# One fused attention and feed-forward kernel on one core: whole result tiles in one transfer, reciprocals on VectorE, one QK tile in batch 0, and another searched order

## The chip, the cores and the metric

The kernel runs on one core of one Trainium2 chip. The time is the device time of one execution in microseconds (us). The core's engines are named as in the profile: PE is TensorE (PEld its weight loads), DVE is VectorE, ACT is ScalarE, POOL is GpSimd, and SP is SyncE, which computes nothing here and issues transfers.

## What is computed

Attention with mixing over the heads ahead of the softmax and behind it, and then a feed-forward layer with a squared ReLU:

```python
scores = scale * np.matmul(q, k.transpose(0, 1, 3, 2))     # 8 batches, 12 heads, 448 x 448, d = 64
scores = np.einsum('bhij,hg->bgij', scores, w_pre)         # 12 x 12
attn = softmax(scores)                                     # max, exp, sum, divide
attn = np.einsum('bhij,hg->bgij', attn, w_post)
attn_out = np.matmul(attn, v)
x = attn_out.transpose(0, 2, 1, 3).reshape(B * S, H * D)   # 3584 x 768
h = np.maximum(x @ w_in, 0.0)                              # 768 x 2048
out = (h * h) @ w_out                                      # 2048 x 768
```

## The kernel before, in words

All matmuls are bf16 and accumulate in eight PSUM banks, the one tile `ps`. A batch passes through these stages, each a chain of PE work and of evictions that ACT or DVE makes:

- **T** (line 833 in batch 0, 837 after it): q and k are transposed on PE and evicted into `qkt`.
- **QK** (975 and 985): 128 query rows of all twelve heads at a time are multiplied with the keys and evicted into `stage`, twelve evictions of 128x448 to a tile. SP then regroups `stage` into `dring` by transfers (`emit_rel`, line 1030): one slot of `dring` is a chunk of ten query rows with its 12 heads, 120 partitions. A batch has 45 chunks, handled in 23 pairs.
- In batch 0 the first `ND = 30` chunks go another way (`emit_spr`, line 916): q is spread out with zeros (`qz`, which lies in `h2t`), and PE makes the chunk directly, with eight matmuls on 32 columns each and one eviction into `dring`. The rest of batch 0's rows are `NQ0 = 2` QK tiles (`QT0`), of 70 and 78 rows, each computed as 128 rows.
- **pre** (1054, 1061, 1069): the pair is mixed with `w_pre`. ACT takes `exp` from PSUM (line 1094) into `pring` and leaves the row sums. A reciprocal of the row sums follows (`t_rec`, 1117 on POOL, where it is a power of -1 with the constant tile `minus1`; 1119 on DVE in the first five pairs), and POOL folds it into the weights of the second mixing (`t_fold`, 1127, `wk2s`).
- **post** (1159): the pair is mixed with `wk2s`; two evictions go into `a2t`.
- **AV** (1216, 1237): times v, evicted into `xt`.
- **F1** (1288, 1296): times `w_in`, then ReLU from PSUM into `h1t` (1333 on ACT, 1334 on DVE), squared by DVE into `h2t` (1343).
- **F2** (1427, 1435, and 1375 for the last two tiles): 128 rows times `w_out`, two evictions into `osb`, and the tile leaves for `out`. The two halves of a tile are 64 positions each, so SP issues one transfer to a half (`fn_od`, line 1473); the last two tiles leave by quarters (1398), some of them issued by ACT.

Every stage but the first may run while others wait: attention of one batch is mixed with F1 and F2 of the batch before. What comes when on PE is a string, `ORDER`. Each character takes the next unit of one stream (0 to 9: T, QK, pre, post, AV, the direct chunks, two streams of F1, two of F2), and characters from a letter on also choose a form. A unit of F1 or F2 can be done with halves of the rows of the array (64x128, two at a time), with the whole array (128x128, half as many matmuls), or with quarters (64x64, twice as many); QK and pre have two forms. `_Plan.run` replays that string against a cost model when the program is built. In it DVE, ACT and POOL take whatever is ready first, evictions go to ACT or DVE by which is free, each PE unit gets the PSUM banks that come free first, a change of form costs `MODE_SWITCH`, and blocks of `BLOCK = 256` PE instructions have to be fetched (`FETCH`). What comes out is a fixed order of instructions on each engine, with semaphore waits; the engines run it in that order. So the constants of the model move instructions, and they cost no time themselves.

At the end the kernel looks whether all row sums were in range (lines 1540 to 1560): three DVE operations, a transfer of 128 numbers (`goods`), a last DVE operation (`flag`). Every engine reads `flag` behind its last task and branches: a second program with a safe softmax follows if the flag is 0 (`emit_engine`).

Of the kernel before, what the change touches and what calls it, by code (L numbers as in the profile page):

```python
# [7 lines left out]
ALU = mybir.AluOpType  # L8
# [14 lines left out]
FETCH = (2700.0, 2300.0, 1500.0)  # L23
# [3 lines left out]
DMA_END = {"move": 1450.0, "load": 1300.0}  # L27
# [3 lines left out]
    "0000511100551155555555555555555c2155555035bcb02515525353c2c5155c1531333355c2555c355332c0"  # L31
    "240443c4b200gh1111h62b3g33hqc31cgc3h2b3hgh3bbbch3633r3gb42444223g1h72qgqb2733g1r12q713h3"
    "6b2673722392003t122j33t2b282bi338333s04202444bb002gqbb28311i313s111s322gh2227hqh3613q1hr"
    "3363q2422444br2br631q1731h613q32h0220gh22qg373r3c38212i3s333814144420022ghh20028118111i1"
    "33s339b22j31t22193229119313t3319242444312q2bq227373163c3631731h2020q1g2br2h236333q20b0r2"
    "r20038318311i33184bb42244229c19311t133t118222833i313s242444232q2b623713733631g12r2br2006"
    "33q33rb17q200262r217293c3t331t2200jc181118133s311842244422391319313t13392422444222838333"
    "i311i31qb2b62qb2622h73733373q1b6rb00h2q0202q22h700239331911j11193182238318331s2424442228"
    "1s311i333814244413bq22g2rb2r23631q32r2br23633g31r002h2633q733r024044412tb2j0209bb2t23811"
    "381138333s11t22jb2922t23831s33i1318b4244422bq2bqb27337631q33731r2q21q2r22h1633673373bs22"  # L40
    "842i2i244422383833s333s22qr6r22293933t33tq4q444hghh6gq7g6hrghisrggh7hg7giqishhjjijtsttsj"
    "j"
# [330 lines left out]
def bass_talking_heads_attention__then__ffn_squared_relu_kernel(  # L373
# [18 lines left out]
    ND = 30  # L392
    NE = 6
    NQ0 = 2
# [21 lines left out]
    with ExitStack() as es:  # L416
# [34 lines left out]
        minus1 = sb("minus1", [128, 2, 1], DT.float32)  # L451
# [41 lines left out]
        def program(guard):  # L493
# [40 lines left out]
            def fn_init(eng, en):  # L534
# [8 lines left out]
                eng.memset(minus1[:, :, :], -1.0)  # L543
# [479 lines left out]
            def emit_rel(b, c, n, r0, d0, nv):  # L1023
# [4 lines left out]
                def fn(eng, en):  # L1028
# [5 lines left out]
                             {SP: (1000.0, 0.0)}, g * 1.0, sem, 16,  # L1034
# [51 lines left out]
            def after_pre(g, t_pre, gr, x):  # L1086
# [28 lines left out]
                def fn_rec(eng, en):  # L1115
                    if en == POOL:
                        return eng.tensor_tensor(rinv[:, p0:p0 + n, :], rowsum[:, g0:g0 + n, :],  # L1117
                                                 minus1[:, 0:n, :], ALU.pow)
                    return eng.reciprocal(rinv[:, p0:p0 + n, :], rowsum[:, g0:g0 + n, :])
# [286 lines left out]
            def emit_F2(b, tile, s, s_F):  # L1406
# [61 lines left out]

                o_free[s] = []
                for x, (p0, n_p, row, step) in enumerate(pieces):  # L1470
                    def fn_od(eng, en, p0=p0, n_p=n_p, row=row, step=step):
                        dst = bass.AP(out.tensor, row * F, [[step * F, n_p], [1, F]])
                        eng.dma_start(dst, osb[p0:p0 + n_p, s, :]).then_inc(sem_out[s].handle, 16)

                    o_free[s].append(plan.add("odma%d_%d_%d" % (b, tile, x), SP, fn_od, evs,
                                              {SP: (720.0, 0.0)}, b * 1000.0 + 710, sem_out[s], 16,
                                              dma=("move", 50.0 + 12.0 * n_p, 200.0)))
# [58 lines left out]
            if not guard:  # L1536
# [26 lines left out]
                t_flag = add("flag", DVE, fn_flag, [t_turn], {DVE: (200.0, 300.0)}, 1e8)  # L1563

# [59 lines left out]
        def emit_engine(eng_name, eng):  # L1624
            tasks = fast[eng_name]
            k = len(tasks)
            while k and tasks[k - 1].name == "final":
                k -= 1
# [3 lines left out]
            with eng.If(fine == 0):  # L1632
                emit_tasks(eng_name, eng, tasks[k:], fast_waits)
# [3 lines left out]
            if k < len(tasks):  # L1637
# [51 lines left out]
```

## Time and profile before

| | us |
|---|---|
| median of 3 runs | 534.45 |
| lowest and highest | 530.79, 538.87 |
| the profiled execution | 531.75 |
| its span, first to last instruction | 530.1 |
| granted PE clock | 0.996 |

| engine | busy us | share of the span |
|---|---|---|
| PE | 504.9 | 95% |
| ACT | 429.9 | 81% |
| DVE | 387.7 | 73% |
| POOL | 292.6 | 55% |

How to read it: the span is 1.65 us shorter than the execution's own time. A busy PE is not a PE at its peak, since the matmuls overlap and their ends are modelled: what a unit really takes is read from the start of one group of matmuls to the start of the next. Idle time "before" a group is what the profile shows as free behind the modelled end of the group ahead of it, so a stall is some tenths of a us longer from start to start than the idle time that is printed. "issue" is time in which an engine waited for nothing that the profile shows.

### The profile page before, as it was taken

The page shows a single profiled execution, that of the slowest core. Times are in us where ns is not written, and L with a number is a line of the kernel's source. Part 1 is how long each engine was busy: PE and PEld are TensorE (multiplying, and loading weights), DVE is VectorE, ACT ScalarE, POOL GpSimd, SP SyncE. Part 2 cuts the span into 40 slices and gives each one's busy share as a digit, 9 for nine tenths or more (in the row PEclk, how much of TensorE's full clock was granted, in tenths as well). Part 3 has the DMA queues.
Part 4 walks back from the last instruction along what each step waited for, and adds up shares of the span by engine and source line. Part 5 has one row for each costly group of instructions (what it writes and reads, how often), then busy time and mean ns, then how long its engine had stood idle before and what let it go on. Part 6 is the DMA issues. An engine that isn't in the chain of part 4 may idle for free.

```text
span 530.1 us, 24988 instructions
## 1 busy us (share of the span) xinstructions
PE 504.9 (95%) x10519; PEld 329.4 (62%) x10519; DVE 387.7 (73%) x816; ACT 429.9 (81%) x1223; POOL 292.6 (55%) x524
## 2 busy tenths in 40 slices
PE   8999999999999999999899989999999999999994
PEld 4446776668765655666566655566666665678862
DVE  7898987889886699867787667776888668555400
ACT  5999989889978798888798878978978878977420
POOL 9847788527944597258752576416964445442000
PEclk9999999999999999999999999999999999999998
DMA  9999999646965799458954699536992567531022
GB/s 165 197 201 172 181 192 183 140 96 138 180 147 117 158 167 185 101 113 155 176 115 96 126 196 151 119 64 146 181 176 55 124 139 145 113 93 35 1 57 70
DMA packets 81811, 71.10 MB, mean 134 GB/s; under 512 B 13610, under 2 KB 78234, under 8 KB 81690
## 3 DMA queue, kind: packets, MB, share of 16 engines
q1 hardware_dynamic: 48138, 46.62, 36.1%
q0 software_dynamic: 33392, 22.59, 31.3%
q8 instruction: 86, 1.41, 1.1%
q14 instruction: 35, 0.29, 0.2%
q10 hardware_dynamic: 160, 0.20, 0.1%
HBM read 45.63 MB, written 11.01 MB: 107 GB/s over the span
## 4 chain that ended last, share of the span: by engine, by line
PE 72%; ACT 15%; POOL 7%; DVE 2%; issue 2%; DMA 1%; ACTq 0%; POOLq 0%
PE ps L1435 23%; PE ps L1296 13%; PE ps L1288 7%; PE ps L1159 7%; ACT pring L1094 6%; PE ps L1069 5%; PE ps L1237 5%; PE ps L985 4%; ACT stage L524 4%; POOL rinv L1117 3%; PE ps L1375 2%; PE ps L1427 2%; ACT dring L524 1%; POOL wk2s L1127 1%; PE ps L975 1%
## 5 line engine op out<-in xcount | busy, mean ns | idle before, releaser
L1117 POOL TENSOR_TENSOR rinv<-rowsum,minus 128x2 f32<-128x2 f32 (+1 forms) x179 | 126.1, 706 | 174.7 <-ACT pring L1094 173.9
L1094 ACT ACTIVATE pring<-ps 128x448 bf16<-128x448 f32 x360 | 192.3, 562 | 12.0 <-PE ps L1069 9.4
L525 DVE CAST a2t<-ps 128x480 bf16<-128x480 f32 (+1 forms) x205 | 124.8, 641 | 31.6 <-PE ps L1159 30.6
L1435 PE MATMUL ps<-w_out_sb,h2t 64*128 64x384 bf16 (+1 forms) x1728 | 141.4, 323 | 0.5 <-issue 0.4
L525 DVE CAST stage<-ps 128x448 bf16<-128x448 f32 (+1 forms) x193 | 115.0, 617 | 25.8 <-PE ps L985 15.1
L1296 PE MATMUL ps<-xt,w_in_sb 64*64 64x448 bf16 (+4 forms) x1872 | 121.0, 327 | 1.8 <-issue 1.2
L524 ACT ACTIVATE a2t<-ps 128x480 bf16<-128x480 f32 (+1 forms) x163 | 87.6, 581 | 22.5 <-PE ps L1159 21.7
L1435 PEld LDWEIGHTS ps<-w_out_sb,h2t 64*128 64x128 bf16 (+1 forms) x1728 | 74.6, 97 | 45.1 <-issue 1.9
L524 ACT ACTIVATE stage<-ps 128x448 bf16<-128x448 f32 (+1 forms) x167 | 87.0, 549 | 14.3 <-PE ps L985 9.6
L1296 PEld LDWEIGHTS ps<-xt,w_in_sb 64*64 64x64 bf16 (+1 forms) x1872 | 65.0, 102 | 34.5 <-issue 2.5
L1094 ACT ACTIVATION_READ_ACCUMULATOR pring<-ps 128x1 f32 x360 | 81.6, 227 | 0.0
L1127 POOL TENSOR_TENSOR wk2s<-wk2b,rinv 128x120 bf16<-128x120 bf16 (+1 forms) x179 | 70.7, 396 | 12.4
L1159 PEld LDWEIGHTS ps<-wk2s,pring 60*128 60x128 bf16 x2880 | 56.6, 93 | 31.9 <-DVE a2t L525 4.8
L1159 PE MATMUL ps<-wk2s,pring 60*128 60x60 bf16 x2880 | 64.8, 187 | 6.9 <-POOL wk2s L1127 4.2
L1343 DVE TENSOR_TENSOR h2t<-h1t 128x448 bf16<-128x448 bf16 (+2 forms) x176 | 53.3, 331 | 23.3 <-ACT h1t L1333 22.5
L1069 PE MATMUL ps<-dring,wk 64*64 64x448 bf16 (+1 forms) x622 | 54.5, 359 | 2.6 <-ACT h1t L1333 0.9
L1333 ACT ACTIVATE h1t<-ps 128x448 bf16<-128x448 f32 (+2 forms) x93 | 40.4, 439 | 14.4 <-PE ps L1288 5.9
L1334 DVE TENSOR_SCALAR h1t<-ps 128x448 bf16<-128x448 f32 (+2 forms) x83 | 41.3, 505 | 11.4 <-PE ps L1296 8.4
L1288 PE MATMUL ps<-xt,w_in_sb 128*128 128x220 bf16 (+2 forms) x420 | 47.4, 265 | 0.2
L1288 PEld LDWEIGHTS ps<-xt,w_in_sb 128*128 128x128 bf16 x420 | 38.2, 98 | 7.3 <-ACT pring L1094 0.9
L985 PE MATMUL ps<-qkt 64*128 64x448 bf16 (+1 forms) x288 | 39.5, 353 | 1.4 <-DVE a2t L525 0.8
L738 POOL DMA_DIRECT2D vraw<-in_v_dram x54 | 34.3, 640 | 0.0
(76 smaller groups left out, 434.2 us busy)
## 6 DMA issues: line engine op xcount, KB each, us to landing
dring<-stage SPq DMA_DIRECT2D x301, 105.0 KB
out_dram<-osb SPq DMA_DIRECT2D x45, 192.0 KB, 3.6
qraw<-in_q_dram POOLq DMA_DIRECT2D x42, 112.0 KB, 5.0
kraw<-in_k_dram POOLq DMA_DIRECT2D x42, 112.0 KB, 5.1
w_in_sb<-in_moe_w_in_dram POOLq DMA_DIRECT2D x8, 384.0 KB, 10.2
w_out_sb<-in_moe_w_out_dram POOLq DMA_DIRECT2D x8, 384.0 KB, 8.9
vraw<-in_v_dram POOLq DMA_DIRECT2D x21, 128.0 KB
vraw<-in_v_dram POOLq DMA_DIRECT2D x21, 96.0 KB
```

The source lines that it names most:

```text
L524: return eng.activation(o, i_, AF.Copy)
L525: return eng.tensor_copy(o, i_)
L985: r_ = eng.matmul(ps[y * w:(y + 1) * w, g.banks[x], 0:S], qkt[r0:r0 + 64, pb, p + y, 0, i0:i0 + w], qkt[r0:r0 + 64, pb, p + y, 1, :], star ...
L1069: r_ = eng.matmul(ps[64 * y:64 * y + 64, gr.banks[x], 0:S], wk1[64 * x:64 * x + 64 - R0 * x, 64:128], dring[64 * x:64 * x + 64 - R0 * x, ( ...
L1094: return eng.activation(pring[:, pr, 0:S], ps[:, gr.banks[x], 0:S], AF.Exp, accum_out=rowsum[:, g, :])
L1117: return eng.tensor_tensor(rinv[:, p0:p0 + n, :], rowsum[:, g0:g0 + n, :], minus1[:, 0:n, :], ALU.pow)
L1127: return eng.tensor_tensor(wk2s[:, p0:p0 + n, :], i0.to_broadcast([128, n, PR]), rinv[:, p0:p0 + n, :].to_broadcast([128, n, PR]), ALU.mult)
L1159: r_ = eng.matmul(ps[:, gr.banks[x], o0:o0 + PR], pring[64 * x:64 * x + PR, pr + y, j0:j0 + 2 * PJ], wk2s[64 * x:64 * x + PR, pr + y, :], ...
L1288: r_ = eng.matmul(ps[:, g.banks[ph], 0:n], w_in_sb[:, ft, t * 128:(t + 1) * 128], xt[:, ft, c0:c1], start=(ft == 0), stop=(ft == NFT - 1))
L1296: r_ = eng.matmul(ps[z:z + w, g.banks[x], 0:n], w_in_sb[64 * y:64 * y + 64, ft, t * 128 + z:t * 128 + z + w], xt[64 * y:64 * y + 64, ft, c ...
L1343: return eng.tensor_tensor(h2t[:, t16, o0:o0 + n], h1t[:, s, 0:n], h1t[:, s, 0:n], ALU.mult)
L1435: r_ = eng.matmul(ps[z:z + w, g.banks[hh], 0:FH], h2t[64 * y:64 * y + 64, t16, col + z:col + z + w], w_out_sb[64 * y:64 * y + 64, t16, hh ...
```

## The change

- **Result tiles.** From batch 1 on a result tile leaves by one transfer of 2 x 64 rows in place of two of 64, except for the tiles that join two batches, and except for the last two tiles.
- **Reciprocals.** All are on DVE; the power on POOL and its constant are gone. The fold stays on POOL.
- **Batch 0.** `ND` is 32 and `NQ0` is 1: two more chunks are made directly, and one QK tile of 128 rows is left.
- **The flag.** ACT and SP read it and branch as soon as it is there, in the middle of their last stage; what they still have to do stands behind the branch in both of its ways. PE, DVE and POOL read it last, as before.
- **The order.** Another string, and with it other constants in the model.

```diff
-FETCH = (2700.0, 2300.0, 1500.0)
+FETCH = (4000.0, 0.0, 0.0)
-DMA_END = {"move": 1450.0, "load": 1300.0}
+DMA_END = {"move": 1700.0, "load": 1300.0}
 ORDER = (
-    "0000511100551155555555555555555c2155555035bcb02515525353c2c5155c1531333355c2555c355332c0"
...
+    "000b55555100555555015555555155555b2c552c55555533100223552c25355535c23555300bcc5551325333552"
...
-    ND = 30
+    ND = 32
-    NQ0 = 2
+    NQ0 = 1
...
                 def fn_rec(eng, en):
-                    if en == POOL:
-                        return eng.tensor_tensor(rinv[:, p0:p0 + n, :], rowsum[:, g0:g0 + n, :],
-                                                 minus1[:, 0:n, :], ALU.pow)
                     return eng.reciprocal(rinv[:, p0:p0 + n, :], rowsum[:, g0:g0 + n, :])

-                t_rec = add("rec%d_%d" % (b, c), DVE if g < 10 else POOL, fn_rec,
-                            [exp_of[g0], t_exp] + old_users(g),
-                            {DVE: (82.0, 160.0), POOL: (120.0, 180.0)}, b * 1000.0 - 900 + c)
+                t_rec = add("rec%d_%d" % (b, c), DVE, fn_rec, [exp_of[g0], t_exp] + old_users(g),
+                            {DVE: (82.0, 160.0)}, b * 1000.0 - 900 + c)
...
+                whole = b and not (b % 2 and tile == 3)
                 o_free[s] = []
-                for x, (p0, n_p, row, step) in enumerate(pieces):
+                for x, (p0, n_p, row, step) in enumerate(pieces[:1] if whole else pieces):
                     def fn_od(eng, en, p0=p0, n_p=n_p, row=row, step=step):
-                        dst = bass.AP(out.tensor, row * F, [[step * F, n_p], [1, F]])
-                        eng.dma_start(dst, osb[p0:p0 + n_p, s, :]).then_inc(sem_out[s].handle, 16)
+                        if whole:
+                            dst = bass.AP(out.tensor, row * F, [[F, 2], [step * F, n_p], [1, F]])
+                            i_ = osb[:, s, :]
+                        else:
+                            dst = bass.AP(out.tensor, row * F, [[step * F, n_p], [1, F]])
+                            i_ = osb[p0:p0 + n_p, s, :]
+                        eng.dma_start(dst, i_).then_inc(sem_out[s].handle, 16)
...
+                for en in (ACT, SP):
+                    plan.add("turn" + en, en, None, [t_flag], {en: (3600.0, 3600.0)}, -1e8)
...
-            while k and tasks[k - 1].name == "final":
-                k -= 1
+            for i, t in enumerate(tasks):
+                if t.name == "turn" + eng_name:
+                    k = i
+            rest = tasks[k + 1:]
             emit_tasks(eng_name, eng, tasks[:k], fast_waits)
...
             with eng.If(fine == 0):
-                emit_tasks(eng_name, eng, tasks[k:], fast_waits)
+                emit_tasks(eng_name, eng, rest, fast_waits)
...
-            if k < len(tasks):
+            if rest:
                 with eng.Else():
-                    emit_tasks(eng_name, eng, tasks[k:], fast_waits)
+                    emit_tasks(eng_name, eng, rest, fast_waits)
```

What the build makes of it can be counted in the instruction lists of the two programs (the way that a good flag chooses):

| | before | after |
|---|---|---|
| PE matmuls | 10519 | 9813 |
| PE instructions (a weight load and a matmul each, and waits) | 21630 | 20217 |
| changes of the array's form along PE's list | 222 | 310 |
| F1: matmuls on 64x64, 64x128, 128x128 | 1200, 672, 420 | 624, 360, 720 |
| F2: matmuls on 64x64, 64x128, 128x128 | 384, 1344, 128 | 384, 1024, 288 |
| QK: matmuls on 64x64, 64x128 | 228, 204 | 304, 154 |
| direct chunks: matmuls on 128x32 | 240 | 256 |
| evictions into `stage`, 128 rows (DVE and ACT) | 276 | 264 |
| evictions into `dring` (DVE and ACT) | 30 | 32 |
| reciprocals on DVE, powers on POOL | 5, 179 | 184, 0 |
| SP transfers to `out`: two halves in one, 64 rows, 32 rows | 0, 45, 14 | 20, 5, 14 |
| SP transfers into `dring` | 359 | 357 |

More of the change, by code (lines that the diff above doesn't have):

```diff
@@ L450, in bass_talking_heads_attention__then__ffn_squared_relu_kernel @@
         rinv = sb("rinv", [128, NPS, 1], DT.float32)
-        minus1 = sb("minus1", [128, 2, 1], DT.float32)
         sb("align", [128, 64], DT.uint8)
@@ L542, in fn_init @@
                 eng.memset(rowsum[:, NCP - 1::NCP, :], 1.0)
-                eng.memset(minus1[:, :, :], -1.0)
                 return eng.memset(ident[:, :], 0.0)
@@ L1033, in emit_rel @@
                 t = plan.add("rel%d_%d_%d" % (b, c, d0), SP, fn, sev_of[n],
-                             {SP: (1000.0, 0.0)}, g * 1.0, sem, 16,
+                             {SP: (950.0, 0.0)}, g * 1.0, sem, 16,
                              dma=("move", 10.0 + 73.3 * nv, 54.0))
```

28 lines of the change are left out of this document (15 added, 13 removed).

## Prediction

> **What bounds the kernel now.** I read the page first, then PE's waits, then PE's timeline from start to start, then the rows of the work that changes.
>
> ```profile
> span 530.1 us, 24988 instructions
> PE 504.9 (95%) x10519; PEld 329.4 (62%) x10519; DVE 387.7 (73%) x816; ACT 429.9 (81%) x1223; POOL 292.6 (55%) x524
> q8 instruction: 86, 1.41, 1.1%
> PE 72%; ACT 15%; POOL 7%; DVE 2%; issue 2%; DMA 1%; ACTq 0%; POOLq 0%
> ```
> PE is the bound: 95% busy, and most of the chain that ended last. It is idle for 530.1 - 504.9 = 25.2 us. The stages say where:
>
> ```profile
> 0.00:20.00 20.00, 17.90 (x293) 9.07 (x297) 14.78 (x49) 13.03 (x27) 18.82 (x38) 1.00 1.09 174
> 20.00:60.00 40.00, 37.81 (x814) 20.88 (x807) 36.81 (x80) 39.60 (x123) 26.50 (x45) 1.00 1.08 186
> 460.00:531.00 71.00, 62.28 (x939) 46.13 (x930) 22.00 (x59) 33.73 (x97) 12.85 (x24) 0.96 0.22 53
> ```
> The columns behind the stage are busy us of PE, PEld, DVE, ACT, POOL. From 20 to 60 us ACT is busy 39.60 of 40 and DVE 36.81: there the evictions bound, and PE lost 2.1 + 2.2 = 4.3 us up to 60 us. In the last stage PE lacks 8.7 us, 0.9 of it because the stage is cut wider than the span, and the rest behind its last matmul:
>
> ```profile
> 522.39 0.49 ACT L524 ACTIVATE osb<-ps 128x384 f32<-128x384 f32 x1 [2.11 <-PE ps L1375]
> ```
> PE ends at 522.4, so 530.1 - 522.4 = 7.7 us are the tail. That leaves 25.2 - 7.7 = 17.5 us inside, of which the waits name these:
>
> ```profile
> PE ps L1159 <- POOL wk2s L1127: 4.2, 5, 1.3
> PE ps L661 <- DVE warm L646: 1.4, 1, 1.4
> PE ps L1296 <- issue: 1.2, 1, 1.2
> ...
> PE ps L837 <- issue: 0.7, 2, 0.5
> PE ps L985 <- issue: 0.5, 1, 0.5
> PE ps L1159 <- issue: 0.4, 1, 0.4
> PE ps L1435 <- issue: 0.4, 1, 0.4
> PE ps L1069 <- issue: 0.3, 1, 0.3
> ```
> So: 4.2 us for the folded weights, 3.5 us "issue" in 7 waits, 1.4 us at the start, and about 8 us of many small waits for evictions. The rest of PE's time is work and changes of form.
>
> **The change, part by part.**
>
> *Changes of form, 222 to 310.* Their price is read from start to start:
>
> ```profile
> 116.34 1.30 PE L1288 MATMUL ps<-xt,w_in_sb 128*128 128x220 bf16 x12
> 117.57 0.76 PE L1069 MATMUL ps<-dring,wk 64*64 64x448 bf16 x10
> 118.26 2.44 PE L1288 MATMUL ps<-xt,w_in_sb 128*128 128x220 bf16 x24
> 120.63 0.40 PE L1159 MATMUL ps<-wk2s,pring 60*128 60x60 bf16 x16
> ```
> Twelve whole-array matmuls take 117.57 - 116.34 = 1.23 us, twenty-four 120.63 - 118.26 = 2.37. The twelve more cost 1.14, so a piece that ends in another form costs 1.23 - 1.14 = 0.09 us beyond its work. Elsewhere sixteen half matmuls take 1.41 us behind another form and 1.30 without:
>
> ```profile
> 476.52 1.41 PE ps L1435 x16
> 478.15 1.30 PE ps L1435 x16
> 502.40 1.30 PE ps L1427 x8
> ```
> That is 0.11. I take 0.10: 88 x 0.10 = +8.8 us, between 88 x 0.09 = 7.9 and 88 x 0.11 = 9.7. All of it is on PE, nothing covers it. The last row shows that the form itself is free: eight whole matmuls take the 1.30 of sixteen halves. [...]
>
> *Fewer PE instructions, 21630 to 20217.* The 86 packets of the instruction queue carry 1.41 MB, 16.4 KB each, and 21630 / 86 = 251: each brings about 256 PE instructions. Where a block is used up before the next has come, PE stands:
>
> ```profile
> 389.09 0.36 PE L1296 MATMUL ps<-xt,w_in_sb 64*128 64x448 bf16 x2
> 390.62 1.12 PE L1296 MATMUL ps<-xt,w_in_sb 64*128 64x448 bf16 x10 [1.17 <-issue]
> ```
> From start to start that is 1.53 us for two matmuls that need 0.19, so 1.34 lost where 1.17 is printed. With some 0.2 us more in each of the 7, the 3.5 us are about 5. Priced with rates such as the 1.30 us above, 26 of the old list's 84 blocks of 256 are shorter than 5 us, and 11 of the new list's 78. I scale: 5 x (1 - 11/26) = -2.9 us; bounds 0 and -5.
>
> *Reciprocals to DVE.*
>
> ```profile
> L1117 POOL TENSOR_TENSOR rinv<-rowsum,minus 128x2 f32<-128x2 f32 x171 | 121.7, 713 | 174.1 <-ACT pring L1094 173.3
> L1119 DVE RECIPROCAL rinv<-rowsum 128x2 f32<-128x2 f32 x5 | 0.8, 152 | 0.0
> 143.05 0.70 POOL L1117 TENSOR_TENSOR rinv<-rowsum,minus 128x2 f32<-128x2 f32 x1
> 143.71 0.67 POOL L699 DMA_DIRECT2D qraw<-in_q_dram  x1
> 144.41 0.40 POOL L1127 TENSOR_TENSOR wk2s<-wk2b,rinv 128x120 bf16<-128x120 bf16 x1
> 144.95 0.40 PE L1159 MATMUL ps<-wk2s,pring 60*128 60x60 bf16 x16 [0.89 <-POOL wk2s L1127]
> ```
> POOL loses 122 us of work in these 171. The way from exp to fold is shorter by 713 - 152 = 0.56 us, and POOL, which also issues loads (0.67 us between power and fold here), is no longer behind. The five waits are 4.2 us printed, about 5.2 from start to start. Most were such late folds (estimate); I take -4.0, between 0 and -5.2. On DVE 179 more reciprocals are 179 x 0.152 = 27 us: 388 to about 408 us (77%) with the evictions that go, below. That is hidden as long as DVE's evictions come in time. If that cover is gone, each late eviction holds a PSUM bank and PE (first rival). Queued behind a reciprocal that waits for ACT's exp are DVE's evictions, and PE waits for those.
>
> *One QK tile less in batch 0.* It removes twelve evictions, adds two.
>
> ```profile
> L525 DVE CAST stage<-ps 128x448 bf16<-128x448 f32 x148 | 87.5, 617 | 21.9 <-PE ps L985 12.2 <-PE ps L975 8.0 <-issue 0.8
> L524 ACT ACTIVATE stage<-ps 128x448 bf16<-128x448 f32 x128 | 66.4, 553 | 12.0 <-PE ps L985 7.9 <-PE ps L975 2.6 <-DMA dring<-stage 1.1
> ```
> Ten evictions of about 0.585 are 5.9 us less on ACT and DVE together, where the reciprocals of batch 0 add 18 x 0.152 = 2.7: 3.2 us less, 1.6 on each. There ACT and DVE bound, so I take -1.5 of the 4.3 us that PE lost up to 60 us (bounds 0 and -4.3). PE's own columns change by about -0.5 us.
>
> *The order's other waits.* Between the last write into a PSUM bank and its next use the old list has less than 1.5 us of PE work in 312 of 1444 cases, the new in 284 of 1436. A little looser: I take -2.0 of the remaining 8 us and what their starts hide (bounds -8 and +8: another order has its own waits).
>
> *Whole result tiles.*
>
> ```profile
> L1473 SPq DMA_DIRECT2D out_dram<-osb x59: 422/597/1752, 96.7 to 515.6; - x59
> SPq L1030 <- PE ps L985: 29.1, 19, 18.2
> ```
> SP issues 20 transfers in place of 40: 20 x 0.6 = 12 us of issuing go. SP's queue is not among PE's waits above, so 0; the work that hides it is PE's. Without cover, a transfer into `dring` behind it would come 0.6 us earlier.
>
> *The flag.*
>
> ```profile
> L1632 SPq COMPARE_BRANCH  x1: 50/50/50, 525.1 to 525.1; - x1
> L1574 SPq EVENT_SEMAPHORE  x2: 17/22/28, 528.3 to 528.4; - x2
> L1398 SPq DMA_DIRECT2D out_dram<-osb x6: 466/597/1787, 512.5 to 523.4; - x6
> DMA to landing us min/median/max: 2.1/2.5/4.2
> ```
> SP branches at 525.1 and goes on at 528.3. Its last transfer is issued at 523.4 and lands 2.1 to 4.2 us later, by 527.6 at the latest. So the branch, not the landing, ends last, by 0.7 us or more (up to 2.8): -0.6, since the end of ACT and the barrier still follow. In the middle of the last stage ACT now stands for such a branch, some 3 to 4 us; it is busy for 33.7 of 71 us there, and DVE 22.0, so I take 0, with +3 as the other bound.
>
> *The sum* against the profiled execution: 531.75 + 8.8 - 2.9 - 4.0 - 1.5 - 0.5 - 2.0 - 0.6 = 529.05. That execution lies 2.7 us below the median of 534.45, inside 530.79 to 538.87; with runs that lie so far apart I forecast **529** and do not add the difference.
>
> **The rivals.**
>
> *DVE blocks (slower).* POOL waited for exp 173.9 us in 62 waits:
>
> ```profile
> POOL rinv L1117 <- ACT pring L1094: 173.9, 62, 8.2
> ```
> On DVE, in a fixed order, such waiting stands in front of evictions. If each of the 179 moved reciprocals delays PE by 0.095 us, that is 17 us: 529 + 17 = **546**. It decides from (545.1 - 529) / 179 = 0.09 us each, 2% above the median. For it: ACT is the late engine. Against it: DVE is idle for 142 us.
>
> *Nearly all stalls go (faster).* PE's 17.5 us inside with 0.2 us hidden in each of some 25 waits are about 22. If the new order leaves 2 of them: 531.75 + 8.8 - 0.5 - 20 - 0.7 = 519.35, **519**. For it: longer blocks, shorter way to the fold. Against it: the looser bank uses are few.
>
> *Only the changes of form count.* PE's waits move elsewhere and stay as long: 531.75 + 8.8 - 0.5 = **540**. This is what would follow where the change doesn't do what it says: the new transfers and reciprocals hide nothing that PE waits for. [...]
>
> **How the numbers follow.** The forecast (529, own range 521 to 538) has 0.36, nearly all stalls gone 0.31, only the changes of form 0.13, DVE blocks 0.20. A measurement of this kernel can tell about 2% from no change: 523.8 to 545.1. Faster by over 2% is the 0.31 and 0.06 of the forecast's low end, 0.37. Within 2% is 0.30 and 0.13, 0.43. Slower is 0.20. The range 513 to 543 takes in the 519, the 529 and the 540 with their spread, and leaves out most of DVE blocks and a little below.
>
> **What the new profile would show.** Right: five or fewer PE waits on `wk2s` with under 1 us together; PE "issue" near 2 us; F1 and F2 pieces still 0.1 us longer wherever the form changes; DVE near 408 us; POOL near 170; SP's branch near 485 us, and its last wait ended by a landing. Wrong: DVE waiting for ACT's exp at the reciprocal line for tens of us with PE waits on DVE evictions behind them; new PE waits of several us around the flag; or PE idle as much as before while its busy time falls.

## The result, and the profile after

The changed kernel takes **614.8 us** (median of 4 runs, 608.2 to 619.1); the kernel before, on the same chips, 534.6 (4 runs). The ratio is 1.149 with a 95% interval of 1.134 to 1.163. Here and below a median is over all executions, while a ratio leaves out those in a slower state, over 1.5% above the fastest of their kernel. The forecast of 529 with its range of 513 to 543 is far off, and 615 lies far beyond the slower rival of 546 too.

The profiled execution took 616.29 us. Its page begins so (busy us and share of the span of each engine, then the granted PE clock in 40 slices, then the chain that ended last, by engine and by line):

```profile
span 614.4 us, 23483 instructions
...
PE 534.0 (87%) x9813; PEld 331.9 (54%) x9813; DVE 397.2 (65%) x988; ACT 427.0 (69%) x1219; POOL 167.1 (27%) x345
...
PEclk9998999999979779989998788999799959998997
...
PE 56%; DMA 29%; ACT 8%; DVE 4%; issue 2%; SPq 0%; ACTq 0%; POOL 0%; DVEq 0%
DMA dring<-stage 14%; DMA out_dram<-osb 13%; PE ps L1281 11%; PE ps L1428 10%; PE ps L1289 8%; PE ps L1066 5%; PE ps L1152 5%; PE ps L1420 4%; PE ps L1230 3%; ACT pring L1091 3%; PE ps L982 2%; ACT stage L522 2%; DMA goods<-good 2%; PE ps L972 1%; PE ps L834 1%
```

Read it against the page of before. PE is idle for 614.4 - 534.0 = 80.4 us where it was 25.2: +55.2. PE is also *busy* 534.0 - 504.9 = 29.1 us longer, although it has 706 matmuls fewer. And DMA, which held 1% of the chain, holds 29%: half of it transfers into `dring`, half of it result tiles. The clock, at 9 in all slices but the last before, falls below 9 in thirteen, to 7 or 5 in seven of them.

The waits of the changed kernel (us in total, times, longest) say who is late. In such a row the first engine waits, with what it would write, for what stands behind the arrow:

```profile
ACT osb L522 <- DMA out_dram<-osb: 45.6, 6, 13.6
DVE osb L523 <- DMA out_dram<-osb: 29.4, 4, 13.3
PE ps L1066 <- DMA dring<-stage: 24.7, 5, 6.5
PE ps L982 <- DVE osb L523: 12.4, 1, 12.4
DVE flag L1556 <- DMA goods<-good: 9.4, 1, 9.4
PE ps L1152 <- POOL wk2s L1120: 0.2, 1, 0.2
```

ACT and DVE wait 45.6 + 29.4 = 75.0 us to write into `osb`, since the tile that was there two tiles earlier has not left (`osb` has two slots). While they stand, no PSUM bank comes free, and PE stands too (12.4 us in one wait for an eviction of DVE into `osb`, the fourth row). PE's waits for `dring` are new. The last row is the one term that came out as forecast: PE waits 0.2 us for the folded weights, where it was 4.2.

One stretch in order of time (start, duration, engine, line, what, and in brackets the idle time ahead with its releaser; some rows of all engines):

```profile
166.29 2.34 SPq L1471 DMA_DIRECT2D out_dram<-osb  x3
...
168.73 17.68 SPq L1027 DMA_DIRECT2D dring<-stage  x13
...
180.34 0.59 PE L1066 MATMUL ps<-dring,wk 64*64 64x448 bf16 x4 [6.50 <-DMA dring<-stage]
...
180.86 2.74 PE L1428 MATMUL ps<-w_out_sb,h2t 64*128 64x384 bf16 x16
...
184.64 1.46 PE L1428 MATMUL ps<-w_out_sb,h2t 64*128 64x384 bf16 x16
```

A result tile goes out, and behind it on the same queue stand the transfers into `dring`: SP needs 17.68 us to issue thirteen of them, and PE stands 6.5 us for one. When PE starts again, sixteen matmuls take 2.74 us; four us later sixteen of the same line take 1.46. The granted clock is 0.50 from 180 to 184 us, behind the long idle time. Most of the 29 us of busy time are from such stretches: with each tile in two halves (first run below) PE is busy 516.0 us, 18.0 less. The other 11 come with the rest of the change. So these waits are paid twice: behind each of the eleven waits of PE of 2.66 to 12.36 us in this trace the granted clock is 0.50, until 3.6 to 6.9 us past the end of the wait. The chain of waits over this stretch names both kinds of transfer (start, us, what):

```profile
169.64 10.45 DMA dring<-stage
...
189.04 12.98 DMA dring<-stage
...
207.62 16.09 DMA out_dram<-osb
```

Why does a tile take so long? In the last stage the loads are over, and one whole tile leaves almost alone. The columns behind the stage are busy us of PE, PEld, DVE, ACT, POOL, the granted clock, the mean busy share of 16 DMA engines, and GB/s:

```profile
568.00:576.50 8.50, 8.50 (x75) 7.58 (x74) 2.75 (x10) 3.87 (x11) 0.00 (x0) 0.88 0.13 46
```

0.13 of 16 engines is 2. The packet records say the same: the tile is 128 packets of 3072 bytes, and for 8.1 of its 9.2 us exactly two are under way. The destination of the whole tile is `[[F, 2], [step * F, 64], [1, F]]`: its outermost dimension is 2. The bytes are the same as those of two halves, whose outermost dimension is 64.

### The profile page after: what moved, and what is told of

Its sections match the earlier page's. It is cut to its first block, busy times and chain, and to the rows that moved or that the text cites. A ratio compares the mean times of both kernels' runs of the same rounds, so it can differ in the third digit from the quotient of the medians.

```text
span 614.4 us, 23483 instructions
## 1 busy us (share of the span) xinstructions
PE 534.0 (87%) x9813; PEld 331.9 (54%) x9813; DVE 397.2 (65%) x988; ACT 427.0 (69%) x1219; POOL 167.1 (27%) x345
## 4 chain that ended last, share of the span: by engine, by line
PE 56%; DMA 29%; ACT 8%; DVE 4%; issue 2%; SPq 0%; ACTq 0%; POOL 0%; DVEq 0%
DMA dring<-stage 14%; DMA out_dram<-osb 13%; PE ps L1281 11%; PE ps L1428 10%; PE ps L1289 8%; PE ps L1066 5%; PE ps L1152 5%; PE ps L1420 4%; PE ps L1230 3%; ACT pring L1091 3%; PE ps L982 2%; ACT stage L522 2%; DMA goods<-good 2%; PE ps L972 1%; PE ps L834 1%
## 5 line engine op out<-in xcount | busy, mean ns | idle before, releaser
L523 DVE CAST stage<-ps 128x448 bf16<-128x448 f32 (+1 forms) x184 | 110.3, 617 | 35.5 <-PE ps L972 15.2
L1428 PE MATMUL ps<-w_out_sb,h2t 64*128 64x384 bf16 (+1 forms) x1408 | 118.1, 338 | 0.0
L1281 PE MATMUL ps<-xt,w_in_sb 128*128 128x228 bf16 (+2 forms) x720 | 104.6, 297 | 6.3 <-DVE h1t L1327 2.9
L1066 PE MATMUL ps<-dring,wk 64*64 64x448 bf16 (+1 forms) x632 | 57.6, 380 | 37.0 <-DMA dring<-stage 24.7
L1281 PEld LDWEIGHTS ps<-xt,w_in_sb 128*128 128x128 bf16 x720 | 67.2, 101 | 36.3 <-issue 6.4
L1428 PEld LDWEIGHTS ps<-w_out_sb,h2t 64*128 64x128 bf16 (+1 forms) x1408 | 61.6, 102 | 38.3 <-issue 5.9
L1152 PEld LDWEIGHTS ps<-wk2s,pring 60*128 60x128 bf16 x2880 | 54.5, 95 | 28.6 <-ACT pring L1091 6.2
L1289 PE MATMUL ps<-xt,w_in_sb 64*64 64x448 bf16 (+3 forms) x984 | 68.6, 339 | 0.4 <-ACT h1t L1326 0.3
L522 ACT ACTIVATE osb<-ps 128x384 f32<-128x384 f32 x35 | 17.1, 490 | 70.8 <-DMA out_dram<-osb 45.6
L1066 PEld LDWEIGHTS ps<-dring,wk 64*64 64x64 bf16 (+1 forms) x632 | 18.6, 107 | 59.1 <-issue 32.4
L1113 DVE RECIPROCAL rinv<-rowsum 128x2 f32<-128x2 f32 (+1 forms) x184 | 28.7, 156 | 30.8 <-ACT pring L1091 30.1
L1289 PEld LDWEIGHTS ps<-xt,w_in_sb 64*64 64x64 bf16 (+1 forms) x984 | 34.6, 104 | 22.1 <-issue 1.9
```

What stands on the lines that cost most here:

```text
L522: return eng.activation(o, i_, AF.Copy)
L523: return eng.tensor_copy(o, i_)
L1066: r_ = eng.matmul(ps[64 * y:64 * y + 64, gr.banks[x], 0:S], wk1[64 * x:64 * x + 64 - R0 * x, 64:128], dring[64 * x:64 * x + 64 - R0 * x, ( ...
L1152: r_ = eng.matmul(ps[:, gr.banks[x], o0:o0 + PR], pring[64 * x:64 * x + PR, pr + y, j0:j0 + 2 * PJ], wk2s[64 * x:64 * x + PR, pr + y, :], ...
L1281: r_ = eng.matmul(ps[:, g.banks[ph], 0:n], w_in_sb[:, ft, t * 128:(t + 1) * 128], xt[:, ft, c0:c1], start=(ft == 0), stop=(ft == NFT - 1))
L1289: r_ = eng.matmul(ps[z:z + w, g.banks[x], 0:n], w_in_sb[64 * y:64 * y + 64, ft, t * 128 + z:t * 128 + z + w], xt[64 * y:64 * y + 64, ft, c ...
```

## The experiments

**Three theories.** W: the outermost dimension of 2 puts the tile on two of the sixteen transfer engines; it lands some 10 us late, keeps `osb` (two slots) and holds up the transfers into `dring` behind it. R: the reciprocals on DVE and the new order do it. S: a transfer of 384 KB as such is too large. Four kernels tell them apart.

*The changed kernel with the whole tile in two transfers of 64 rows, issued by the same task.*

```
-  if whole:
-      dst = bass.AP(out.tensor, row * F, [[F, 2], [step * F, n_p], [1, F]])
-      i_ = osb[:, s, :]
...
+  for y in range(2 if whole else 1):
+      dst = bass.AP(out.tensor, (row + y) * F, [[step * F, n_p], [1, F]])
+      i_ = osb[p0 + 64 * y:p0 + 64 * y + n_p, s, :]
+      eng.dma_start(dst, i_).then_inc(sem_out[s].handle, 16)
...
```

> The changed kernel, all of it, but each of its 20 whole tiles leaves by two transfers of 64 rows, issued one behind the other by the same task; every other instruction stands where it stood. Theory W (the destination of the whole transfer has 2 as its outermost dimension, and such a transfer runs on few of the 16 DMA engines, so that it lands some 10 us late and holds osb and the transfers into dring behind it): about 529 us, which was the forecast of the sum without it, between 515 and 545, the waits of ACT and DVE for out_dram<-osb (75.0 us) below 2, PE clock at 0.99. Rival R (the reciprocals on DVE or the new order are the cause): 590 us or more, with the granted clock still near 0.94. Rival S (384 KB in one transfer is too much, whatever its form) also says 529 here.

Measured: 543.2 us, ratio 1.017 (1.011 to 1.023). Of the 80 us, 72 are gone with this edit alone: 54.4 of PE's idle time (80.4 to 26.0) and 18.0 of its busy time. No wait for `osb`'s transfers is left. What is left, 10 us, is the subject of the later runs. One part of it is in this row, of which the kernel before has none:

```profile
PE ps L1066 <- DMA dring<-stage: 5.9, 3, 2.8
```

Two of these waits, 2.8 us each at 201 and 445 us, have 3.4 us at a clock of 0.50 behind them. What makes these transfers late with two halves was not tried.

*The kernel before with only the whole transfer.* Order, reciprocals, flag and QK tiles stay as before.

```
+  whole = b and not (b % 2 and tile == 3)
...
+  if whole and x == 0:
+      return None
+  if whole:
+      dst = bass.AP(out.tensor, (row - 1) * F, [[F, 2], [step * F, n_p], [1, F]])
+      eng.dma_start(dst, osb[:, s, :]).then_inc(sem_out[s].handle, 16)
+      return None
...
```

> The kernel before with one thing of the change: its 20 whole tiles leave by the whole transfer of 2 x 64 rows, issued where the second half was; the first half's place stays empty. Theory W: much slower, 580 to 630 us, ACT and DVE waiting for out_dram<-osb for tens of us, pre waiting for dring<-stage. Rival R: 535 us, as the kernel before.

Measured: 599.1 us, ratio 1.124 (1.116 to 1.132). One part of the change, put alone into the old kernel, costs 66 us. Here too ACT and DVE wait for `osb`'s transfers, 24.1 + 48.2 us, and PE 18.9 us for `dring`. R falls for the bulk.

*The outermost dimension in doses.* One transfer for each whole tile, same bytes and sizes, but rows at other places of the output (so these four kernels give another output and serve the timing alone), with an outermost dimension of 2, 4, 8 and 16:

```
-  dst = bass.AP(out.tensor, row * F, [[F, 2], [step * F, n_p], [1, F]])
+  dst = bass.AP(out.tensor, at * F, [[F, 16], [16 * F, 8], [1, F]])     # or [F, 2], [2 * F, 64]; [F, 4], [4 * F, 32]; [F, 8], [8 * F, 16]
...
```

> The changed kernel, its result rows put side by side in the output (a whole tile's 128 lanes go to 128 neighbouring rows, the other tiles' rows also side by side, so the rows of the output are in other places). Outermost dimension 2: rows x + 2p, x of 2, p of 64. This is the control for the next run. Theory W and rival S: as slow as the changed kernel, 600 to 625 us. A rival by which the row distance of 7 x 3072 bytes is the cause: 525 to 545.

> As the run before, the same bytes in one transfer into the same 128 neighbouring rows, with 16 as the outermost dimension: rows x + 16p, x of 16, p of 8 (lanes go to other rows than in the run before). Theory W: near the run with two halves, 515 to 545 us, a landing some 3 us after the issue. Rival S (size): 600 us or more, as with 2.

> The changed kernel, one transfer for each whole result tile, with an outermost dimension of 4 at the output (rows go to other places of the output; bytes, rows and sizes stay). The theory that the outermost dimension sets how many transfer engines carry the tile: each tile takes about half as long as with 2, so it lands some 5 us later than a well spread one instead of 10, and the time lies between 540 and 570 (2 gave 615, 16 gave 537). The rival that any value but 2, or any order of the rows other than the two far halves, is as good as 16 gives 535 to 539.

> The same with an outermost dimension of 8. By the number of transfer engines the tile takes a quarter of what it takes with 2, some 2.5 us more than with 16, so 536 to 545; by the rival 535 to 539. What tells them apart is the duration of the tile's 128 packets in the trace: near twice that of 16 and half that of 4 by the theory, equal to 16 by the rival.

| outermost dimension | time, us | ratio (95%) | ACT and DVE wait for `osb`'s transfers, us |
|---|---|---|---|
| 2 | 615.3 | 1.152 (1.142 to 1.161) | 44.8 + 28.6 = 73.4 |
| 4 | 568.5 | 1.067 (1.059 to 1.075) | 20.5 + 9.9 = 30.4 |
| 8 | 546.3 | 1.026 (1.019 to 1.033) | 2.1 + 1.5 = 3.6 |
| 16 | 536.8 | 1.003 (0.999 to 1.007) | none |

The same stretch of the last stage, one tile almost alone, in the runs with 4, 8 and 16 (the row for 2 stands above):

```profile
526.50:533.50 7.00, 7.00 (x55) 6.06 (x54) 2.65 (x10) 3.25 (x10) 0.00 (x0) 0.77 0.21 55
```

```profile
506.00:510.00 4.00, 4.00 (x45) 4.00 (x43) 2.15 (x9) 2.55 (x8) 0.00 (x0) 1.00 0.42 102
```

```profile
499.50:501.70 2.20, 2.20 (x27) 2.20 (x25) 1.33 (x6) 1.35 (x5) 0.00 (x0) 1.00 0.69 182
```

The share goes 0.13, 0.21, 0.42, 0.69. In the packet records of the same four tiles 2, 4, 8 and 16 packets are under way at once while the transfer is at its fullest, and the tile leaves in 9.2, 7.7, 4.3 and 1.8 us. From 2 to 4 the time does not halve, as a run's expectation had it: a packet takes 192 ns on average there and 141 with 2; why is not shown. The kernel's time follows the dose. With 2 it is 615.3 us, as in the changed kernel, so the distance of the rows in the output is not the cause. S falls: at 16, 384 KB in one transfer cost nothing that can be told from before. That the waits grow faster than the landing (0, 3.6, 30.4, 73.4 us) fits the two slots of `osb`: a tile that leaves in 4 us is nearly always gone in time, one that needs 9 us and queues behind others is not.

One transfer for a tile is not bad as such: with 16 the kernel takes 536.8 us, 6.4 less than with two halves on the same order, and the two intervals of the ratio do not touch. PE's waits for `dring` are 2.9 us there and 5.9 with two halves. The output's own layout was not tried with a well spread whole tile.

**The terms of the sum, one by one, on the kernel before.**

*All reciprocals on DVE.*

```
-  t_rec = add(..., DVE if g < 10 else POOL, fn_rec, ...
+  t_rec = add(..., DVE, fn_rec, ...
```

> The kernel before with one edit: every reciprocal goes to DVE, as in the changed kernel; order, transfers and the rest stay. The theory that the outermost dimension of the result transfer explains the loss, and that the prediction's term for the reciprocals (-4.0) was right, gives 533.3 - 4 = about 529 to 531, with PE's waits on wk2s under 1 us (4.2 before) and POOL near 170 us busy. The rival that DVE's blocked queue costs the changed kernel its remaining 10 us gives about 540 to 546, with PE waits behind DVE's evictions.

Measured: 527.7 us, ratio 0.991 (0.987 to 0.995): -4.9 us. In the profile DVE is 400.9 us busy and POOL 168.1, and no wait of PE for `wk2s` is left. DVE's blocked queue costs nothing that shows.

*The early branch on the flag.*

```
+  for en in (ACT, SP):
+      plan.add("turn" + en, en, None, [t_flag], {en: (3600.0, 3600.0)}, -1e8)
...
```

> The kernel before with one edit: ACT and SP branch on the flag as soon as it is known and not at the end. The prediction's term (-0.6) gives 532 to 533.5, SP's branch about 40 us before the end and SP's last wait ended by a landing; the tail from the last matmul to the end shorter by 1 to 2.5 us if the branch was what ended last. The rival that ACT's early branch delays evictions gives 535 to 538 with PE idle for some us around the flag.

Measured: 528.9 us, ratio 0.992 (0.989 to 0.995): -4.2 us, more than was forecast.

```profile
L1636 SPq COMPARE_BRANCH  x1: 50/50/50, 489.5 to 489.5; - x1
```

SP branches 40 us ahead of the end. In the profiled execution of before, the last packet of a result ends at 527.1 and the span at 530.1; here at 529.0 and 529.9. So the way from the last landing to the end is 2 us shorter. From PE's last matmul to the end it is 7.7 us before and 4.8 here. The rest of the 4.2 is not accounted for.

*Both together.*

> The kernel before with the two parts of the change that gained: all reciprocals on DVE and the early branch on the flag; old order, two half transfers. If the parts add, 533 x 0.9908 x 0.9921 = 524 (521 to 527). If both gains are only different timings of the same waits, 527 to 530. The rival that DVE's queue becomes tight with both gives 531 or more.

Measured: 529.8 us, ratio 0.995 (0.992 to 0.998). The gains do not add: -2.7 together, where -4.9 and -4.2 stand alone. Blocks of instructions that come late (below) are the likely reason: PE's waits named "issue" in this run are

```profile
PE ps L1296 <- issue: 5.0, 4, 2.0
PE ps L1159 <- issue: 2.6, 2, 1.9
PE ps L837 <- issue: 2.1, 2, 1.1
```

9.7 us, where they were 3.5 in the kernel before. But the profile of the reciprocals alone, an execution 8 us above that run's median, has 7.2 us of them too, so this is not settled. These three runs, reciprocals, flag and both, are the ones below the kernel before; which of them is best can't be told from their intervals.

*More changes of form.* Neighbouring pieces of PE's order are exchanged by one or two places until the form changes 210 times more often; nothing else.

```
-  ORDER = ("0000511100551155555555555555555c2155555035bcb025...")
+  ORDER = (218 of its 969 places exchanged with a neighbour one or two places away)
```

> The kernel before with neighbouring pieces of PE's order exchanged (by one or two places) so that the form of the matmuls changes 210 times more often; pieces, loads, transfers and engines stay. The prediction's price of 0.10 us for each change gives 533.3 + 21 = 554 (from 0.09 and 0.11: 552 to 556). The rival that most changes hide behind waits for evictions or blocks, so that the term of 8.8 was too large, gives under 544; the rival that a change costs nearer 0.15 us gives over 564.

Measured: 550.9 us, ratio 1.035 (1.029 to 1.041). 550.87 - 532.93 = 17.9 us for 210, so 0.085 us for each (0.07 to 0.10 by the interval). PE's busy time shows the same: 524.5 - 504.9 = 19.6 us, 0.093, and its idle time is 24.7 us, as before.

*The new order alone.* The kernel before with the changed kernel's order, its constants of the model and its one QK tile in batch 0.

```
-  ORDER = (before's)
+  ORDER = (the changed kernel's)
...
-  ND = 30
+  ND = 32
...
-  NQ0 = 2
+  NQ0 = 1
```

> The kernel before with the changed kernel's order and its one QK tile in batch 0, and nothing else of the change: reciprocals on POOL, flag at the end, two half transfers with a task each. The prediction's terms that belong to the order (+8.8 - 2.9 - 1.5 - 0.5 - 2.0 = +1.9) give 533 + 1.9 = 535. The theory that the order itself is what the remaining 10 us of the changed kernel with two halves are made of (543.2, with reciprocals and flag that were measured at -4.9 and -4.1 on the old order) gives 543 + 9 = about 552, and at least 545; PE's stalls then exceed those of before by 8 us or more beside the changes of form. A result near 543 means that reciprocals and flag gain nothing on the new order.

Measured: 539.8 us, ratio 1.013 (1.007 to 1.018): +7.3 us where the terms gave +1.9. The page:

```profile
span 538.5 us, 23499 instructions
...
PE 514.3 (96%) x9812; PEld 322.1 (60%) x9812; DVE 378.3 (70%) x800; ACT 432.0 (80%) x1229; POOL 290.8 (54%) x524
```

PE is busy 514.3 - 504.9 = 9.4 us longer and idle 24.2 us, 1.0 less. Of the 9.4 some 3 are half clock behind one late block (below; 6.8 us at a clock of 0.50); the other 6 are most of what 88 changes of form cost at 0.085 us each, 7.5. Nearly nothing is there of what should have paid for them. With reciprocals and flag besides (the kernel with two halves) it is 543.2, so there those two gain nothing that shows. PE's waits for `wk2s` do fall, from 2.9 us to 0.2, but the 5.9 us for `dring` are new.

**What eats the gains.** The kernel with two halves, PE from 43 to 51 us:

```profile
44.21 0.55 PE L1051 MATMUL ps<-dring,wkf 128*128 128x448 bf16 x2
44.69 0.37 PE L1209 MATMUL ps<-a2t,vraw 64*64 64x220 bf16 x5
48.02 0.40 PE L1209 MATMUL ps<-a2t,vraw 64*64 64x220 bf16 x3 [2.95 <-issue]
```

and the windows behind it:

```profile
44.00:48.00 4.00, 1.06 (x43) 0.41 (x28) 1.67 (x4) 2.31 (x9) 1.03 (x2) 0.89 1.03 194
48.00:50.00 2.00, 1.99 (x10) 0.50 (x11) 1.06 (x3) 0.98 (x2) 0.29 (x1) 0.50 0.65 114
50.00:52.00 2.00, 2.00 (x42) 1.53 (x40) 1.86 (x5) 1.71 (x4) 0.84 (x2) 0.50 0.30 28
52.00:54.00 2.00, 2.00 (x26) 1.99 (x24) 0.70 (x2) 0.99 (x3) 0.00 (x0) 0.51 1.13 161
54.00:56.00 2.00, 2.00 (x46) 1.43 (x43) 0.39 (x1) 1.69 (x5) 0.00 (x0) 1.00 0.64 145
```

PE stops in the middle of a piece, waits for nothing that the profile shows, goes on 1.36 us behind the landing of an instruction block (a packet of the instruction queue, 45.73 + 0.93 = 46.66 us), and then runs for 6 us at a clock of 0.50. That is 3.2 us of waiting (from start to start) and 3 of half speed. The sixteen transfer engines are all busy there (a share of 1.03, 194 GB/s); the loads of `w_out` are among them. The theory: the block's fetch waits behind loads. The rivals: blocks are used up too fast, or the piece waits for its own data. The run with an outermost dimension of 16 and the order alone have the same stall at the same piece.

*The loads of `w_out` twelve chunks later* (and, in a later run, six):

```
-  pre_at(min(24 + 3 * (2 * j + x), NCH - 1))
+  pre_at(min(36 + 3 * (2 * j + x), NCH - 1))      # 30 + 3 * (2 * j + x) in the later run
```

> The changed kernel with two half transfers for each result tile, and the eight loads of w_out each released twelve chunks of batch 0 later; nothing else. The theory that an instruction block comes late because its fetch waits behind loads on the transfer engines gives: the stalls of 1.28 us at 41 us and 3.21 us at 48 us become smaller than 0.5 us together or move to where the loads now are, and the time falls by up to 4 us from 543.2 if they do not come back. The rival that those stalls are due to short blocks (PE uses 256 instructions faster than one block can be fetched) gives the same stalls at the same places and the same time.

Measured: 543.8 us, ratio 1.020 (1.009 to 1.031). From start to start, the 3.21 us became 0.73 and the clock behind it stayed at 1.00, but the 1.28 us at 41 us stayed where it was, against the first expectation. And the loads of queries and keys, which are chained behind those of `w_out`, came late:

```profile
PE ps L834 <- DMA qraw<-in_q_dram: 2.3, 1, 2.3
...
PE ps L834 <- DMA kraw<-in_k_dram: 1.3, 1, 1.3
```

with a clock of 0.50 from 90 to 95 us. The time is the same, so by the time alone this run decides nothing.

> The changed kernel with two half transfers, and the loads of w_out released six chunks later (g6: twelve). In g6 the stall at 48 us fell from 3.21 to 0.73 and its half clock went, but the loads of queries and keys behind them came late at 85 us (2.3 and 1.3 us, half clock again), so the time stayed. Theory: with six chunks the stall at 48 us is under 2 us with the clock at 1.00 behind it, the wait at 85 us is short, and the time is 535 to 540. Rival: the loads have nothing to do with it and the stall of 3.2 us stays, 543.

Measured with six chunks: 537.5 us, ratio 1.011 (1.002 to 1.020). That is 5.7 us below the kernel with two halves, but the intervals of the two ratios overlap, so the time alone does not decide here either. The rows do:

```profile
41.18 0.79 PE L1152 MATMUL ps<-wk2s,pring 60*128 60x60 bf16 x44 [1.09 <-issue]
...
45.54 0.28 PE L1209 MATMUL ps<-a2t,vraw 64*64 64x220 bf16 x3 [0.48 <-issue]
```

The stall is at the same matmul, but 0.48 us long, and the granted clock behind it is 1.00. In both runs PE starts into the block ahead at 41.18 us and uses it up in 3.6 us. The next block lands at 46.66 us with two halves, and at 44.08 here; the share of the transfer engines from 41 to 43 us is 1.14 there and 0.61 here. So the loads are a cause. The length of the block alone, which is the same in both, does not make the long stall; that a longer block would have hidden the late fetch was not tried.

*Block boundaries moved, nothing else.* The first warm-up, where PE has no other work, is cut into more and smaller matmuls, so that every later boundary between blocks of 256 instructions falls earlier in the work:

```
-  for _ in range(n):     # n is 11 in the first warm-up
...
+  big, small = (n - 10, 42) if now < 2000.0 else (n, 0)     # (n - 11, 75) in the second run
+  for x in range(big + small):
+      w = S if x < big else 64
...
```

The first run has 1 + 42 = 43 matmuls in place of 11, so 32 more (9845 on its page against 9813) and not the 31 of its expectation; the second has 64 more.

> The changed kernel with two half transfers for each result tile, and one edit: the first warm-up, while PE has nothing else to do, is made of 1 large and 42 small matmuls instead of 11 large ones. So 31 more matmuls (62 more instructions) pass before the same work, and every boundary between blocks of 256 PE instructions falls 62 instructions earlier in the work. Theory that the 3.2 us at 44.8 us are a block that comes late: that stall is gone from its matmul (the fifth of the piece on L1209) and stands some 62 instructions earlier with another length, with the half clock behind it only if it stays over about 3 us; the time moves with it, 535 to 549. Rival that the wait belongs to that piece of work (its data, its PSUM bank): 3.0 us at the same matmul, half the clock behind it, and 543.

> The same with 75 small matmuls in place of the 11 large: boundaries 128 instructions earlier in the work, half a block. By the theory every stall list of before is void: the stalls that end 1.3 to 1.6 us behind an instruction landing stand at other matmuls, and where no block is late by 3 us the granted clock from 48 to 54 us is 1.00 and the time 535 to 538 (543.2 less the 3.2 and the half of 6 us). By the rival 543 and the stall where it was.

Measured: 539.4 us, ratio 1.007 (1.002 to 1.012), in the first; 543.4, ratio 1.020 (1.012 to 1.027), in the second. In the first the stall is here (the profiled execution took 543.7 us, the slowest of ten; this kernel's line numbers are two higher from 830 on):

```profile
44.97 0.41 PE L836 MATMUL ps<-ident,qraw 64*64 64x64 bf16 x28
45.22 0.20 PE L836 MATMUL ps<-ident,kraw 64*64 64x64 bf16 x4
49.17 0.38 PE L836 MATMUL ps<-ident,kraw 64*64 64x64 bf16 x24 [3.75 <-issue]
49.48 0.55 PE L1053 MATMUL ps<-dring,wkf 128*128 128x448 bf16 x2
49.97 0.38 PE L1211 MATMUL ps<-a2t,vraw 64*64 64x220 bf16 x8
```

It stood behind the fifth matmul of the piece on `a2t,vraw`. Now 24 + 2 + 5 = 31 matmuls lie between its place and that one, and the piece on `a2t,vraw` runs through, eight in a row. Counted in instructions (weight loads, matmuls and semaphore instructions in the trace, in order of time) the two places are the same: 1728 PE instructions lie ahead of the stall in both runs. The clock behind the stall is 0.56 and 0.58 in the windows from 50 to 54 us. That half the clock comes only behind a stall of over about 3 us was the author's estimate, from 3.21 us with it and 1.28 without in the kernel with two halves; in this run an idle time of 2.50 us, ahead of 148.81 us, had it too. In the second run the stall at 48 us is gone, but PE stands at 37.44 us for 3.44 us from start to start, with 1472 instructions ahead, and 1472 is 1728 - 256.

The traces of all seventeen kernels of this case say the same. They have 43 PE waits named "issue" of 1 us or more, and ahead of every one of the 43 stand 256 k + 192 instructions, with PE going on 1.2 to 1.7 us behind the landing of a packet of the instruction queue. So the wait belongs to the block and not to the work: this is shown.

In the second run the half of the expectation that named a time failed: the clock is 1.00 from 48 to 54 us, but with the block at 37.4 us late, a clock of 0.70 from 40 to 44 us and 7.4 us of PE's waits for `dring` the time is 543. Where a block's fetch met the loads went with the place of the boundary in these two runs (a late block at 49.17 us in the one, at 37.44 in the other), and no run put it there by design.

## Why the prediction was wrong, point by point

- **Whole result tiles, costed at 0: the step that failed.** The text reads "SP's queue is not among PE's waits above, so 0". It counted 12 us of issuing on SP and never priced the landing of the transfer, although the diff shows its new outermost dimension. What is in place of the 0: +72 us in the changed kernel (614.8 - 543.2), +66 on the old order. It named a cover, PE's work, and even the one thing behind it, a transfer into `dring` "0.6 us earlier"; in the changed kernel PE stands up to 6.5 us for that transfer, and the chain lies on it for 10.45 and 12.98 us. None of the rivals held this mechanism, and so the range did not reach it. Several of the signs that the text names for being right came true all the same (`wk2s` at 0.2 us, DVE at 397, POOL at 167): they are signs of other terms.
- **Fewer and longer blocks, -2.9: wrong in sign.** PE's waits named "issue" went from 3.5 us in 7 (the kernel before) to 4.6 in 3 with the order alone and 9.0 in 10 with two halves:

```profile
PE ps L1152 <- issue: 3.2, 5, 1.1
PE ps L1209 <- issue: 3.0, 1, 3.0
PE ps L913 <- issue: 1.3, 1, 1.3
PE ps L834 <- issue: 1.1, 1, 1.1
```

The step took a block's length as the only cause, and the 5 us under which it counted a block as short were the author's estimate. The blocks ahead of the long stalls are short indeed (250 PE instructions in 3.5 to 4.5 us with two halves, with the order alone and with moved boundaries), but fewer short blocks in the whole list did not mean fewer stalls: the same short block cost 2.95 us or 0.48, by the loads that its successor's fetch met, and the stall of 3.2 us at 48 us cost 3 more by the clock. The trace of before had no stall over 1.6 us to show that.
- **One QK tile less, -1.5, and looser banks, -2.0.** PE lacked 4.3 us up to 60 us; with two halves it is 60 - 17.05 - 34.94 = 8.0, of which the late blocks at 14.67, 41.18 and 48.02 us are 5.4:

```profile
0.00:20.00 20.00, 17.05 (x284) 8.43 (x285) 14.91 (x49) 11.75 (x21) 18.82 (x38) 1.00 1.09 174
20.00:60.00 40.00, 34.94 (x743) 19.16 (x743) 31.30 (x79) 34.65 (x107) 13.97 (x27) 0.91 1.01 176
```

Without them 2.6 are left, so the first term may hold by itself; no run has it alone. The order alone gave 1.0 us less idle time in all, where these terms with the blocks made 6.4. The bank term was not tried by itself.
- **Changes of form, +8.8: right in kind, a little large.** 88 x 0.085 = 7.5. The rival in which only these count, 540, is close to the order alone (539.8), and to the changed kernel with well spread tiles (536.8), but not for its reason alone: late blocks and half clock are in both.
- **Reciprocals, -4.0: right on the old order (-4.9),** and `wk2s` waits fell from 4.2 to 0.2 us in the changed kernel, as forecast. On the new order with two halves the gain does not reach the end. DVE's 397 us are near the 408 forecast, and POOL's 167 the 170. The rival of a blocked DVE falls: DVE's wait for exp, 30.1 us in the changed kernel and 19.5 with two halves, brings no wait of PE of that size in the latter.
- **The flag, -0.6: right in sign, too small,** -4.2 (2.5 to 5.9) on the old order. In the changed kernel the flag's own small transfer landed 9.4 us after its issue (1.9 before), behind a result tile that was issued 1.0 us ahead of it.

The 615 can now be put together from runs: 533 before, +7 for the order, +3 for the rest with two halves, +72 for the tiles. The +3 is within the noise of its two runs. What stays open is how much of the order's loss is late blocks (some 6 us by the rows above, an estimate: 3 of waiting and 3 of half speed) and how much is waits that another order has by itself, why transfers into `dring` come late with two halves, and why reciprocals and flag do not add.

## What to carry to other kernels

Where a diff merges or reshapes a transfer, price its landing and not its issue: write down the outermost dimension of the destination (46 GB/s with 2 here, 182 with 16), and ask who waits for its buffer and what queues behind it. A gain in small waits counts only once the blocks of instructions are looked at again: with 64 and 128 instructions more ahead of the work their boundaries fell elsewhere in it, and one block that came late cost 3.2 us of waiting and 3 of half speed here, more than any single gain of the sum. To see it, count PE's instructions up to each unexplained wait: here the counts were 256 k + 192 in 43 of 43.

## What was not expected of the hardware

- One transfer of 384 KB with an outermost dimension of 2 had 0.13 of 16 transfer engines and 46 GB/s; with 16 it had 0.69 and 182 GB/s (means over the windows above).
- SP itself stood while it issued transfers behind such a tile, thirteen in 17.7 us, up to 7.6 us for one (the row gives minimum, median and maximum in ns); before, 2.0 was the most.

```profile
L1027 SPq DMA_DIRECT2D dring<-stage x357: 651/934/7565, 29.3 to 533.0; - x179
```

- In the changed kernel the granted clock was 0.50 behind all eleven idle times of PE of 2.66 to 12.36 us, in stretches of 3.4 or 6.8 us, once 13.7; behind idle times of 1.57 and 1.72 us it stayed at 1.00. Half the clock was there behind 2.50 us too, in the first run with moved boundaries (printed as idle ahead of 148.81 us), and with two halves behind 2.95, at 48.02 us.
- A block of 256 PE instructions came so late that PE stood for 3 to 4 us while loads filled the transfer engines (idle for 2.95 us with two halves, where the engines' share was 1.14 ahead of it, and for 3.75 in the first run with moved boundaries, where it was 1.17 from 40 to 44 us; 0.48 where it was 0.61); PE goes on 1.2 to 1.7 us behind the landing, in 43 of 43 waits.
